# Another layout for the first two chunks' alpha, k and q, turned by identity products, with a new order for the opening fifth

## The chip, the cores and the metric

The kernel runs on one core of a Trainium2 chip. The metric is the time of one execution in microseconds (us) of device time. A core has five engines that matter here: TensorE (PE, with its weight loads as PEld), VectorE (DVE), ScalarE (ACT), GpSimd (POOL) and SyncE (SP), which issues the transfers (DMAs). Each engine works through its own instructions in program order and waits for the others by semaphores.

## The reference

A gated linear attention runs over 4 batches, 8 heads, 768 tokens and 48 channels. Its output, put together over the heads to 3072 tokens of 384 channels, goes through a two-layer block with a hardswish.

```python
for t in range(S):                                   # S = 768
    state = alpha[:, :, t, :, None] * state + np.einsum('bhd,bhe->bhde', k[:, :, t], v[:, :, t])
    y[:, :, t] = np.einsum('bhd,bhde->bhe', q[:, :, t], state)
...
x = np.ascontiguousarray(attn_out.transpose(0, 2, 1, 3)).reshape(B * S, H * D)   # 3072 x 384
h = x @ w_in                                         # w_in 384 x 2048
relu6 = np.clip(h + 3.0, 0.0, 6.0)
g = h * relu6 / 6.0
return (g @ w_out).astype(np.float32)                # w_out 2048 x 384
```

The two weight matrices are given as 64-bit floats and reach the kernel as raw bits; the kernel itself makes 32-bit floats of them.

## The kernel before

**Tiling.** The tokens are cut into 24 chunks of 128, six to a batch; chunk `j` belongs to batch `j // 6`. The recurrence within a chunk is done by cumulative products of alpha (scans along the tokens), so alpha, k and q are needed with channels on the partitions and tokens along the row: two heads of 64 rows each (48 channels and 16 rows of padding) fill the 128 partitions, and four such pairs lie side by side. Two chunks make a group of 256 tokens for the two-layer block.

**Loads.** For chunks 0 to 5 (`FIRST = 6`) `load_akq` (L253) brings alpha, k or q of a chunk in one transfer: partition = token, and on it eight heads of 48 channels, each in a place of 64 (L256). The buffers are the three rings of `rings` (L87): ring `j % 3` for chunk `j`. The 16 pad columns of each head are set once at the start, to 1 for alpha and 0 for k and q (L91); ring 0 by VectorE, rings 1 and 2 by GpSimd. From chunk 6 on the loads go another way, through `quads` (L264), four transfers per tensor, and VectorE turns blocks of 32 by 32 (L288).

**Turning.** `transposed` (L276) puts channels on partitions: for each of the four pairs of heads one TensorE transpose of 128 tokens by 128 rows, into one PSUM bank (L284).

**Order.** The kernel writes the order of its work out by hand as one long list of words, each a step of one chunk, group or weight slice, handed to `run` (L768). Each step issues its instructions at once, so the list fixes the order of every engine's instructions and of SP's transfers. The words that matter here, with their engine and line (the number after the dot is the chunk, the slice or the group):

- `la`, `lk`, `lq`: loads of alpha, k, q (SP, L256); `lv`: the two loads of v (SP, L274); `w`: load of one of sixteen weight slices (SP, L162 for the first matrix, L166 for the second)
- `ta`, `tk`, `tq`: the turning (TensorE, L284; from chunk 6 on VectorE, L288)
- `ca`: turned alpha to its place (ScalarE, L302); `r`: scan backwards, with a reciprocal (VectorE, L311, L315); `p`: scan forwards (VectorE, L322); `k`, `q`: k and q times those scans (VectorE, L334)
- `kb`: k back to tokens on partitions (TensorE, L393); `ck`: copy of it (ScalarE, L397); `u`: products for the state (TensorE, L452); `sm`: next state (VectorE, L460, L462); `st`: decayed state (GpSimd, L428); `sv`: state to its place (ScalarE, L438; the first of a batch by a memset on GpSimd); `qa`: q to its place (ScalarE, L385)
- `sc`: scores (TensorE, L365); `m`: masked scores (VectorE, L375); `ya`, `yb`: attention output (TensorE, L478); `cy`: copy of it (ScalarE, L487)
- `d1`, `d2`, `dx` (ScalarE, L186, L196, L191), `d3` (VectorE, L203 to L210), `d4` (GpSimd, L217): the five parts of turning one weight slice into 32-bit floats; `pd`: pads of `quads` (GpSimd, L251)
- `fa`, `fb`, `f`, `fr`, `fg`, `b`: the two-layer block of the first two groups, done directly (TensorE L512, L501, L539; ScalarE L517; VectorE L521)
- `y`, `xc`, `x`, `s` (VectorE) and `M`, `P` (TensorE, L623, L726), `G`, `K`, `n`, `o`: from the second group on, the two matrix products with sums and differences of blocks, which need fewer products
- `z`: products of the identity by itself into an unused PSUM bank, as many as the last number says (TensorE, L555). Nothing reads them. There are 26 of them, all in the opening.

An fp32 product appears in the trace as two matmul instructions; a transpose as one.

The list begins so:

```python
run("""z.0.5 z.0.3 z.0.1 qa.0.0 w.0 d2.0 d3.0 la.0 ta.0.0 z.0.8 lk.0 tk.0.1 la.1 ta.1.2
       lq.0 tq.0.3 lk.1 lv.0.0 d1.0 ca.0 r.0 p.0 k.0 kb.0.0 z.0.2 z.0.2 q.0 la.2 dx.0 ca.1
       r.1 ck.0 u.0.2.1 sm.0.0 qa.0.1 sv.0.1 tk.1.0 p.1 sc.0.2.3 w.2 lq.1 sm.0.1 k.1 m.0
       ta.2.0 z.0.2 d1.2 ca.2 d2.2 kb.1.0 ck.1 r.2 tq.1.2 q.1 dx.2 lv.1.1 u.1.3.1 z.0.3
       ...
       ya.0.3 yb.0 sc.1.0.2 m.1 ...
```

Of the kernel before, what the change touches and what calls it, by code (L numbers as in the profile page):

```python
# [17 lines left out]
def kernel(  # L18
# [32 lines left out]
    nc = tc.nc  # L51
    B, H, S, D = q.shape
# [8 lines left out]
    G = 2  # L61
# [11 lines left out]
    ident = consts.tile([C, C], FP, tag="ident")  # L73
# [8 lines left out]


    NR = 3
    NV = 3
    ring = {}
    rings = consts.tile([C, 3 * NR, H, 64], FP, tag="rings")  # L87
    for r in range(NR):
        for name, pad in (("a", 1.0), ("k", 0.0), ("q", 0.0)):
            t = ring[name, r] = rings[:, 3 * r + "akq".index(name)]  # L90
            (nc.vector if r == 0 else nc.gpsimd).memset(t[:, :, D:64], pad)  # L91

    vs, As = [], []
    for r in range(NV):
        t = consts.tile([C, 2, H, 64], FP, tag=f"v{r}", name=f"v{r}")
# [10 lines left out]
    for r in range(2):  # L106
        t = consts.tile([C, NP * W + 1], FP, tag=f"ax{r}")
        nc.vector.memset(t, 0.0)
        aX.append(t)
        t = consts.tile([C, NP * W], FP, tag=f"ini{r}")  # L110
# [7 lines left out]
    st, half_st, sm = (consts.tile([C, NP, D], FP, tag=name, name=name)  # L118
                       for name in ("st", "s1", "sm"))
# [109 lines left out]
    def bank(name, j, i):  # L229
        ps_t[name, j] = banks[i].rearrange("r (p n) -> r p n", p=NP)  # L230
        return ps_t[name, j]
# [3 lines left out]
    V = C // BLK  # L235
# [3 lines left out]
    for r in range(NQ):  # L239
        for name in "akq":  # L240
            quads[name, r] = consts.tile([C, NP, V, D], FP, tag=f"{name}q{r}",
                                         name=f"{name}q{r}")

    def rows(t, j):
        b, c = divmod(j, NC)
        return t[b, :, c * C : (c + 1) * C, :]
# [5 lines left out]

    def load_akq(name, j):  # L253
        src = rows({"a": alpha, "k": k, "q": q}[name], j)
        if j < FIRST:
            nc.sync.dma_start(out=ring[name, j % NR][:, :, 0:D],  # L256
                              in_=src.rearrange("h s d -> s h d"))
            return
        to = quads[name, j % NQ]
        to = to.rearrange("r p v d -> r p (v d)")  # L260
        t = src.rearrange("(p a) (u v) d -> a u p (v d)", a=2, v=V)
        for o in range(4):
            skip = BLK * (o % 2)
            nc.sync.dma_start(out=to[BLK * o : BLK * (o + 1), :, 0 : V * D - skip],  # L264
                              in_=t[o // 2, :, :, skip : V * D])
# [10 lines left out]
    def transposed(name, j, i=None):  # L276
        if j >= FIRST:
            t = (K_t if name == "k" else Q_t)[j] = (Ks if name == "k" else Qs)[j % 2]
            by_blocks(t, name, j)
            return  # L280
        t = bank("t" + name, j, i)
        src = ring[name, j % NR]
        for p in range(NP):
            nc.tensor.transpose(  # L284
                t[:, p], src[:, 2 * p : 2 * p + 2].rearrange("s h d -> s (h d)"), ident)

    def by_blocks(to, name, j):
        nc.vector.transpose(out=to.rearrange("r p (u v) -> r p v u", v=V),  # L288
                            in_=quads[name, j % NQ][:, :, :, 0:BLK])
# [305 lines left out]
    for i in range(8):  # L595
        r, o = divmod(i, 3)
        spots.append(raws[r].rearrange("p n w -> p (n w)").bitcast(FP)[:, o * QB : (o + 1) * QB])
    xc = consts.tile([C, len(X_SUMS), C], FP, tag="xc")
# [47 lines left out]
    def hidden1(g, o):  # L646
# [16 lines left out]
    b = {(i, k): w2[:, i * HF : (i + 1) * HF, k * HD : (k + 1) * HD]  # L663
         for i in range(2) for k in range(2)}
    spare = rings.rearrange("r n h e -> r (n h e)").rearrange(
        "r (x f n) -> r x f n", x=3, n=HD)
    t = {1: b[0, 1], 2: spare[:, 0], 3: spare[:, 1], 4: spare[:, 2]}
# [76 lines left out]
    def store2(g, i):  # L744
# [5 lines left out]

    steps = {
        "la": lambda j: load_akq("a", j), "lk": lambda j: load_akq("k", j),
        "lq": lambda j: load_akq("q", j), "lv": load_v, "pd": pad, "w": load_weight,
        "d1": round_low, "d2": magnitude, "dx": sign, "d3": high_bits, "d4": add_low,
        "ta": lambda j, *i: transposed("a", j, *i), "tk": lambda j, *i: transposed("k", j, *i),
# [12 lines left out]
    def run(words):  # L768
        for word in words.split():
            name, *at = word.split(".")  # L770
            steps[name](*(int(x) for x in at))

    with tc.manual_schedule():
        run("""z.0.5 z.0.3 z.0.1 qa.0.0 w.0 d2.0 d3.0 la.0 ta.0.0 z.0.8 lk.0 tk.0.1 la.1 ta.1.2
               lq.0 tq.0.3 lk.1 lv.0.0 d1.0 ca.0 r.0 p.0 k.0 kb.0.0 z.0.2 z.0.2 q.0 la.2 dx.0 ca.1
               r.1 ck.0 u.0.2.1 sm.0.0 qa.0.1 sv.0.1 tk.1.0 p.1 sc.0.2.3 w.2 lq.1 sm.0.1 k.1 m.0
               ta.2.0 z.0.2 d1.2 ca.2 d2.2 kb.1.0 ck.1 r.2 tq.1.2 q.1 dx.2 lv.1.1 u.1.3.1 z.0.3
               lq.2 w.1 lk.2 d4.0 lk.3 la.3 la.4 w.3 lq.3 lv.2.2 lk.4 w.5 pd.0 sv.0.0 pd.1 st.1
               sm.1.0 p.2 d3.2 sm.1.1 ya.0.3 yb.0 sc.1.0.2 m.1 d4.2 sv.1.1 cy.0 qa.1.1 sv.1.0 d1.1
               st.2 d2.1 dx.1 fa.0.1 tq.2.1 q.2 tk.2.3 k.2 fa.2.0 sc.2.0.2 d3.1 m.2 d4.1 ta.3.1  # L780
               ta.4.3 kb.2.0 qa.1.0 ca.3 r.3 ca.4 r.4 ya.1.2 yb.1 tk.3.1 fa.1.2 p.3 k.3 qa.2.1
               qa.2.0 cy.1 d2.3 d3.3 fb.2 fb.1 tq.3.1 q.3 sv.2.0 d1.3 ck.2 u.2.3.2 sm.2.0 d4.3
               fr.0.2.0 tk.4.0 d2.5 sv.2.1 k.4 sm.2.1 st.3 fg.0.2 d3.5 w.6 lv.3.0 lq.4 w.7 fb.0
               sc.3.1.3 m.3 kb.3.2 kb.4.0 f.0.3.3 ya.2.1 ck.3 d1.5 d4.5 d1.6 d2.6 d3.6 d4.6 sv.3.0
               qa.3.1 fr.0.1.0 fr.0.3.1 la.5 yb.2 u.3.3.2 sm.3.0 fg.0.3 fg.0.1 sm.3.1 f.0.5.0
               tq.4.3 f.0.6.3 ta.5.2 cy.2 ck.4 d2.7 qa.3.0 d1.7 d3.7 d4.7 fr.0.5.1 fr.0.0.0 sv.3.1
               fg.0.0 fg.0.5 p.4 ya.3.0 yb.3 f.0.7.2 qa.6.0 qa.12.0 qa.18.0 lq.7 w.4 d2.4 cy.3
               fr.0.6.1 w.9 d2.9 ca.5 d1.9 d1.4 dx.4 la.6 w.8 d3.4 lk.5 w.10 d3.9 ca.6 q.4 fg.0.6
               d4.9 w.12 d2.8 st.4 f.1.1.1 f.1.7.0 sc.4.0.2 f.1.3.3 qa.4.0 d1.8 fr.0.7.0 r.6 d3.8
               d4.8 d4.4 fg.0.7 m.4 fr.1.1.0 fr.1.7.1 fg.1.7 fg.1.1 d2.10 d1.10 f.1.0.2 d2.12 d3.10  # L790
               r.5 d4.10 fr.1.0.0 fr.1.3.1 fg.1.3 fg.1.0 d3.12 f.1.6.0 f.1.2.1 la.8 lq.5 lv.4.1
               w.11 w.13 lq.6 u.4.1.0 tk.5.3 sm.4.0 sv.4.0 d1.12 qa.4.1 d4.12 fa.4.3 fr.1.2.0
               fr.1.6.1 d2.11 d2.13 f.1.4.2 d1.11 sm.4.1 fg.1.2 k.5 kb.5.1 tq.5.3 d3.11 p.5 d4.11
               tq.6 fg.1.6 q.5 p.6 d3.13 d1.13 st.5 la.7 w.15 lv.5.0 lk.6 w.14 ck.5 b.0.0.1 fb.4
               ya.4.2 qa.5.1 sv.4.1 yb.4 sc.5.0.3 fr.1.4.1 cy.4 u.5.2 b.0.1 f.1.5.0 fr.0.4.0 d1.15
               sv.5.0 qa.5.0 lv.12.1 lk.7 lv.6.2 sv.12.0 sv.6.0 d4.13 xc.2.0 fg.1.4 q.6 xc.2.2
               sm.5.0 fg.0.4 ca.7 tk.6 sv.5.1 d2.15 d2.14 d1.14 d3.15 fr.1.5.1 d3.14 k.6 d4.14
               d4.15 fg.1.5 m.5 b.0.2 b.1.0.2 b.1.1 kb.6.0 ya.5.3 yb.5 b.1.2 cy.5 P.1.0.0 P.1.1.3
               lq.8 K.1.0 ck.6 u.6.2.3 b.1.3 bo.1 b.0.3 tq.7 y.5 y.1 y.3 y.0 y.6 x.0 y.9 y.7 xc.2.1
               y.11 y.13 y.2 y.8 xc.2.3 x.1 s.1.0.0 s.1.1.1 x.2 tk.7 y.10 s.1.2.3 G.1.0.0 y.4  # L800
               sm.6.0 P.1.3.3 xc.2.4 s.1.3.2 P.1.2 sc.6.2.1 y.16 y.12 y.15 s.1.4 r.7 y.17 y.19
               xc.2.5 y.20 s.1.5 xc.2.7 y.14 y.18 y.21 xc.2.6 y.23 lq.9 so.1 lv.7.0 lk.9 bo.0 K.1.2
               K.1.1 P.1.4 M.2.0.1 P.1.5 n.2.0.8 M.2.1 n.2.1.9 G.1.1.1 M.2.7.2 n.2.7.11 sv.6.1
               sm.6.1 k.7 G.1.2.2 xc.2.10 x.3 xc.2.8 p.7 q.7 st.7 y.22 xc.2.9 m.6 M.2.15.3 M.2.2
               n.2.2.10 M.2.8 kb.7.0 M.2.3 M.2.4 P.1.6 qa.7.0 ck.7 n.2.4.12 G.1.3.3 O.1.0 la.9 lk.8
               ca.9 o.2.0.0 M.2.9 u.7.1.2 ya.6.0 e.2.0.0 qa.6.1 yb.6 lv.8.2 cy.6 y.24 r.9 o.2.1.0
               M.2.10 M.2.5 n.2.10.14 e.2.1.1 n.2.5.13 sm.7.0 h.2.0 tq.8 ca.8 tk.8 h.2.1 M.2.6.0
               M.2.11 M.2.18.1 sc.7.0.3 sv.7.1 qa.7.1 n.2.11.15 n.2.18.10 sv.7.0 M.2.12 M.2.16
               M.2.19 n.2.12.12 M.2.13 sm.7.1 r.8 m.7 o.2.3.0 ya.7.3 n.2.13.12 yb.7 cy.7 M.2.14
# [8 lines left out]
               n.3.11.8 e.3.5.0 M.3.12 n.3.12.10 q.9 O.2.0 kw.9 la.11 kr.8 kr.9 ca.11 up.8.0.1  # L818
               sp.8.2.3 M.3.13 M.3.15.0 M.3.16 G.2.2.0 o.3.3.0 sm.8.0 mp.8 o.3.4.0 sm.8.1 r.10
               sv.8.1 n.3.13.10 M.3.14 P.2.4 o.3.6.1 o.3.7.0 M.3.6.3 qa.8.0 qa.9.0 qa.8.1 sv.8.0  # L820
               st.9 e.3.4.1 lk.11 lq.11 O.1.2 la.12 lq.10 G.2.1.2 P.2.6 sm.9.0 h.3.4 sm.9.1 o.3.2.0
               ya.8.1 sv.9.1 sv.9.0 qa.9.1 st.10 G.2.3.3 yb.8 ya.9.3 yb.9 M.3.17 P.3.0.1 tk.11
               o.3.2.1 o.3.3.1 tk.10 h.3.5 O.2.2 O.2.3 la.13 lv.10.2 sv.10.0 cy.8 e.3.2.1 cy.9
               xc.4.0 xc.4.1 xc.4.3 h.3.2 xc.4.4 xc.4.5 o.3.7.1 M.4.0.0 e.3.6.0 e.3.3.1 h.3.3
               P.3.1.2 e.3.7.1 n.4.0.10 K.3.0 h.3.6 xc.4.6 h.3.7 xc.4.7 k.10 M.4.7.3 M.4.1 n.4.1.13
               tq.10 s.3.1.11 s.3.0.9 G.3.0.0 kt.10 xc.4.8 xc.4.10 s.3.2.12 r.11 p.10 P.3.3.2 M.4.2
               n.4.2.14 n.4.7.15 K.3.2 s.3.3.9 k.11 q.10 s.3.5 kt.11 p.11 s.3.4 P.3.2 M.4.3 M.4.4
# [128 lines left out]
```

## Time and profile before

| | |
|---|---|
| median of 3 runs | 530.81 us (529.37 to 530.86) |
| the profiled execution | 530.19 us, of which its span 528.4 us |
| TensorE busy | 519.6 us, 98% of the span |
| VectorE busy | 471.7 us, 89% |
| ScalarE busy | 257.9 us, 49% |
| GpSimd busy | 49.7 us, 9% |
| moved by DMA | 54.40 MB; 83,328 of 124,100 packets under 512 bytes |
| first load of alpha | issued at 1.24 us, landed 5.48 us later |
| first scan on VectorE | starts at 8.59 us |

Times in the trace count from the start of the span. The timeline lists instructions in order of time, with the idle time of the engine before them and what ended it. The chain of waits is followed back from the last instruction: at each step to what released it, or to the instruction before it on its engine. A table by stretches gives each engine's busy time within a window. A matmul's duration holds its way through the array; matmuls follow one another faster than that, so work is counted by the spacing of instructions in a full stream.

### The profile page before, as it was taken

The numbers are of one execution on the slowest core, as the hardware profiler recorded it, in microseconds if no ns is written. First come the engines' busy times: TensorE is split into PE (matmuls) and PEld (weight loads), VectorE is DVE, ScalarE is ACT, GpSimd is POOL, SyncE is SP. The second block draws the span as 40 slices with busy tenths as digits, with TensorE's granted clock in tenths as the row PEclk, the third lists the DMA queues.
The fourth block names the chain that finished last, engine by engine and source line by source line (L and its number), as shares of the span: only waits on it lengthen the run. The fifth ranks groups of instructions, "written<-read, shape, count | busy, mean of one in ns | idle before, by whom it ended". The sixth has DMA issues, their size and how long they took to land.

```text
span 528.4 us, 15020 instructions
## 1 busy us (share of the span) xinstructions
PE 519.6 (98%) x6300; PEld 495.6 (94%) x6300; DVE 471.7 (89%) x817; ACT 257.9 (49%) x503; POOL 49.7 (9%) x71
## 2 busy tenths in 40 slices
PE   7899999999999999999999999999999999999997
PEld 7788887779999999999999999999999999999997
DVE  6999999999999999999999999999999996276471
ACT  4889866013653643652544536543444545344330
POOL 6323342100000000000000100000000000000000
PEclk9999999999999999999999999999999999999999
DMA  9999987140026535355555453454163150010001
GB/s 173 222 254 265 245 242 170 29 119 1 17 58 140 131 84 120 78 110 125 123 114 133 98 117 75 111 120 118 30 139 92 30 121 13 2 31 8 9 1 45
DMA packets 124100, 54.40 MB, mean 103 GB/s; under 512 B 83328, under 2 KB 116864, under 8 KB 124032
## 3 DMA queue, kind: packets, MB, share of 16 engines
q1 hardware_dynamic: 124032, 53.44, 44.7%
q8 instruction: 49, 0.80, 0.7%
q14 instruction: 19, 0.16, 0.1%
HBM read 44.50 MB, written 8.91 MB: 101 GB/s over the span
## 4 chain that ended last, share of the span: by engine, by line
PE 81%; DVE 12%; ACT 2%; DMA 2%; issue 2%; POOL 0%; SPq 0%; DVEq 0%; ACTq 0%
PE m_ps L726 37%; PE m_ps L623 35%; PE t_ps L478 4%; PE t_ps L365 2%; PE t_ps L452 2%; DVE g_sb L521 1%; DMA rings<-in_alpha_dram 1%; DVE w L208 1%; DVE raw L210 1%; PE m_ps L555 1%; DVE w L207 1%; DVE P L322 1%; DMA qq<-in_q_dram 1%; DVE A L375 1%; PE t_ps L284 1%
## 5 line engine op out<-in xcount | busy, mean ns | idle before, releaser
L726 PE MATMUL m_ps<-w,g_sb 128*128 128x192 f32 x704 | 121.6, 326 | 0.2 <-DVE oh L742 0.2
L629 ACT COPY g_sb<-m_ps 128x512 f32<-128x512 f32 x110 | 63.5, 585 | 115.4 <-PE m_ps L623 95.1
L726 PEld LDWEIGHTS m_ps<-w,g_sb 128*128 128x128 f32 x704 | 113.8, 190 | 1.2 <-DVE oh L742 0.8
L726 PE MATMUL m_ps<-rings,g_sb 128*128 128x192 f32 x528 | 91.6, 326 | 0.8 <-DVE g_sb L670 0.8
L726 PEld LDWEIGHTS m_ps<-rings,g_sb 128*128 128x128 f32 x528 | 85.3, 190 | 1.1 <-DVE g_sb L670 1.1
L623 PE MATMUL m_ps<-xc,w 128*128 128x128 f32 x640 | 83.5, 278 | 0.0
L517 ACT ACTIVATE r<-g_sb,half 128x512 f32<-128x512 f32 x80 | 56.5, 721 | 49.1 <-DVE g_sb L564 22.8
L623 PEld LDWEIGHTS m_ps<-xc,w 128*128 128x128 f32 x640 | 77.8, 192 | 1.5 <-ACT g_sb L629 0.2
L521 DVE SCALAR_TENSOR_TENSOR g_sb<-r,g_sb 128x512 f32<-128x512 f32 x80 | 53.8, 683 | 4.6 <-ACT r L517 4.4
L623 PE MATMUL m_ps<-xT,raw 128*128 128x128 f32 x400 | 52.2, 276 | 0.0
L623 PEld LDWEIGHTS m_ps<-xT,raw 128*128 128x128 f32 x400 | 48.9, 192 | 0.2
L670 DVE TENSOR_TENSOR g_sb<-g_sb 128x512 f32<-128x512 f32 (+1 forms) x55 | 42.1, 792 | 2.6 <-PE m_ps L726 2.5
L428 POOL TENSOR_TENSOR st<-sm,R 128x192 f32<-128x192 f32 x20 | 12.1, 606 | 337.3 <-DVE sm L462 254.6
L623 PE MATMUL m_ps<-xT,w 128*128 128x128 f32 x320 | 41.7, 276 | 0.0
L623 PEld LDWEIGHTS m_ps<-xT,w 128*128 128x128 f32 x320 | 38.7, 192 | 0.2
L385 ACT COPY A<-q 48x256 f32<-48x256 f32 x88 | 35.5, 403 | 6.0 <-DVE q L334 4.7
L560 DVE TENSOR_TENSOR g_sb<-g_sb 128x512 f32<-128x512 f32 x40 | 27.0, 681 | 6.7 <-ACT g_sb L629 6.6
L501 PE MATMUL m_ps<-xT,w 128*128 128x256 f32 x144 | 32.5, 381 | 0.0
L623 PE MATMUL m_ps<-xc,raw 128*128 128x128 f32 x240 | 32.0, 276 | 0.0
L501 PEld LDWEIGHTS m_ps<-xT,w 128*128 128x128 f32 x144 | 26.9, 190 | 3.8
L311 DVE TENSOR_TENSOR_SCAN R<-t,ones 128x516 f32<-128x516 f32 x24 | 29.5, 1230 | 0.6 <-ACT t L302 0.6
L623 PEld LDWEIGHTS m_ps<-xc,raw 128*128 128x128 f32 x240 | 29.7, 192 | 0.2
(105 smaller groups left out, 722.1 us busy)
## 6 DMA issues: line engine op xcount, KB each, us to landing
raw<-in_moe_w_out_dram SPq DMA_DIRECT2D x8, 768.0 KB, 5.9
raw<-in_moe_w_in_dram SPq DMA_DIRECT2D x6, 768.0 KB, 6.3
v<-in_v_dram SPq DMA_DIRECT2D x48, 96.0 KB, 3.2
out_dram<-oh SPq DMA_DIRECT2D x44, 96.0 KB, 2.0
far<-kq SPq DMA_DIRECT2D x64, 64.0 KB, 2.2
kb<-far SPq DMA_DIRECT2D x64, 64.0 KB, 2.1
qq<-in_q_dram SPq DMA_DIRECT2D x36, 96.0 KB, 2.6
aq<-in_alpha_dram SPq DMA_DIRECT2D x36, 96.0 KB, 2.7
```

Source lines behind the costliest of these rows:

```text
L311: nc.vector.tensor_tensor_scan(out=reverse(R, n - 1, n), data0=reverse(ax, n, n), data1=reverse(ones, n, n), initial=0.0, op0=ALU.mult, op ...
L385: nc.scalar.copy(out=to[:, a], in_=Q_t[j][64 * a : 64 * a + D, :, half])
L428: nc.gpsimd.tensor_tensor(out=st, in0=sm, in1=R_t[j][:, :, 0:1].to_broadcast([C, NP, D]), op=ALU.mult)
L478: nc.tensor.matmul(y_of(j, (i + 1) // 2, p)[:, HB * b : HB * b + HB], vb[:, p, e : e + 32], A_t[j][:, b, 2 * p + a], start=(b == 0 and i = ...
L501: nc.tensor.matmul(h[:, f], w1[:, kk, o : o + C], xT_t[g][:, kk], start=(kk == 0), stop=(kk == KT - 1))
L517: nc.scalar.activation(out=to, in_=h, func=AF.Relu, bias=half, scale=1.0 / 6.0)
L521: nc.vector.scalar_tensor_tensor(out=to, in0=r, scalar=1.0, in1=h, op0=ALU.min, op1=ALU.mult)
L560: eng.tensor_tensor(out=out, in0=in0, in1=in1, op=ALU.add if s1 > 0 else ALU.subtract)
L623: nc.tensor.matmul(acc[g][i][:, f * C : (f + 1) * C], spots[w][:, f * C : (f + 1) * C], x_of(g, x), start=(first and f == 0), stop=last, s ...
L629: nc.scalar.copy(out=slots[z], in_=acc[g][i])
L670: nc.vector.tensor_tensor(out=out, in0=in0, in1=in1, op=ALU.subtract)
L726: nc.tensor.matmul(to[g], a, rhs[:, f], start=(first and f == 0), stop=(last and f == HF - 1), skip_group_check=True)
```

## The change

**Loads.** For chunks 0 and 1 (`QUADS = 2`) a partition now holds four successive tokens of two heads: partition `4u + p` has tokens `4u` to `4u + 3` of heads `2p` and `2p + 1`, so that each run in memory is 4 tokens of 48 channels (768 bytes) instead of one (192 bytes). It is still one transfer per tensor, of 192 KB in all, and fills the first 384 columns of the ring.

**Turning.** For each of the four tokens and each of the two heads of a pair, one fp32 product of 64 columns of the ring (48 channels, and 16 more that lie behind them) with the identity: 64 rows of PSUM by 128 columns, written with a stride of four so that the tokens come out in order. Eight products take the place of four transposes, for alpha, k and q of chunks 0 and 1. The 16 columns behind the last head are set by six more small memsets, three on VectorE and three on GpSimd.

**Order.** The words of the opening (about the first third of the list's text, a fifth of the time) are arranged anew, and `sv.12.0` moves a little further back. The words are the same as before, none more and none fewer.

```diff
+    QUADS = 2
...
             (nc.vector if r == 0 else nc.gpsimd).memset(t[:, :, D:64], pad)
+            if r < QUADS:
+                (nc.vector if r == 0 else nc.gpsimd).memset(t[:, 6, 0:16], pad)
...
     def load_akq(name, j):
         src = rows({"a": alpha, "k": k, "q": q}[name], j)
+        if j < QUADS:
+            to = ring[name, j % NR].rearrange("r h e -> r (h e)")[:, 0 : 2 * V * D]
+            nc.sync.dma_start(out=to.rearrange("r (a x) -> r a x", a=2),
+                              in_=src.rearrange("(p a) (u v) d -> u p a (v d)", a=2, v=V))
+            return
...
         t = bank("t" + name, j, i)
         src = ring[name, j % NR]
+        if j < QUADS:
+            src = src.rearrange("s h e -> s (h e)")
+            for v in range(V):
+                for a in range(2):
+                    o = D * (V * a + v)
+                    nc.tensor.matmul(
+                        t[64 * a : 64 * a + 64].rearrange("r p (u v) -> r v u p", v=V)[:, v],
+                        src[:, o : o + 64], ident, start=True, stop=True)
+            return
...
+        run("""z.0.5 qa.0.0 la.0 ta.0.0 lk.0 tk.0.1 la.1 ta.1.2 z.0.3 ca.0 r.0 k.0 p.0 kb.0.0 ca.1
+               r.1 w.1 lq.0 tq.0.3 z.0.1 lv.0.0 lk.1 la.2 w.0 q.0 lq.1 w.2 lv.1.1 lq.2 lk.2 w.3
+               la.4 la.3 d1.1 ck.0 u.0.2.1 tk.1.0 z.0.8 d2.1 qa.0.1 dx.1 d2.0 d1.0 d3.1 sm.0.0
+               sc.0.2.3 p.1 sm.0.1 k.1 m.0 d3.0 z.0.2 ta.2.0 ca.2 sv.0.1 r.2 z.0.2 tq.1.2 kb.1.0
+               z.0.2 d4.1 st.1 sv.0.0 sv.1.0 ck.1 dx.0 u.1.3.1 sm.1.0 q.1 sm.1.1 p.2 qa.1.1 z.0.3
+               ya.0.3 yb.0 sc.1.0.2 m.1 cy.0 d2.2 d1.2 dx.2 tk.2.3 tq.2.1 q.2 k.2 d3.2 pd.0 d4.0
+               ...
+               P.1.0.0 K.1.0 d4.14 s.1.1.1 tq.6 m.5 y.3 y.6 y.1 k.6 sm.5.0 y.5
+               sv.5.1 s.1.0.0 fg.0.4 y.7 P.1.1.3 b.1.2 b.0.2 b.1.3 ya.5.3 yb.5 kb.6.0 ck.6 y.2
+               s.1.4 s.1.3.2 y.11 x.0 y.4 G.1.0.0 y.16 y.10 y.8 x.1 x.2 s.1.2.3 P.1.2 P.1.3.3 y.0
+               ...
```

## The prediction

> **What bounds the kernel now.** I read the page's busy shares first, then the timeline of the opening, then the chain of waits, then busy time by stretches. The page:
>
> ```profile
> PE 519.6 (98%) x6300; PEld 495.6 (94%) x6300; DVE 471.7 (89%) x817; ACT 257.9 (49%) x503; POOL 49.7 (9%) x71
> PE   7899999999999999999999999999999999999997
> DVE  6999999999999999999999999999999996276471
> ```
>
> TensorE is busy almost throughout, and the holes lie in the first slices. So the end of the program is the moment from which TensorE never stops, plus the work then left. The timeline says when that is (columns: start, duration, engine, line, operation, count, idle time before and its releaser):
>
> ```profile
> 1.24 0.48 SPq L256 DMA_DIRECT2D rings<-in_alpha_dram  x1
> 6.85 1.09 PE L284 MATMUL t_ps<-ident,rings 128*128 128x128 f32 x4 [1.18 <-DMA rings<-in_alpha_dram]
> 7.73 3.23 PE L555 MATMUL m_ps<-ident 128*128 128x128 f32 x16
> 7.97 0.59 ACT L302 COPY t<-t_ps 128x512 f32<-128x512 f32 x1 [0.75 <-PE t_ps L284]
> 8.59 1.23 DVE L311 TENSOR_TENSOR_SCAN R<-t,ones 128x516 f32<-128x516 f32 x1 [0.32 <-ACT t L302]
> ...
> 19.46 0.57 PE L452 MATMUL t_ps<-v,kb 64*48 64x48 f32 x32 [0.29 <-issue]
> 19.96 0.94 PE L555 MATMUL m_ps<-ident 128*128 128x128 f32 x6
> 20.83 1.10 PE L478 MATMUL t_ps<-A,v 128*32 128x64 f32 x64
> 28.63 0.66 PE L393 MATMUL t_ps<-ident,k 128*128 128x128 f32 x4 [0.27 <-DVE A L375]
> ```
>
> Alpha of chunk 0 lands 5.48 us after its issue, and transpose, copy and first scan follow at once. L555 is the filler (`z`). The last filler ends at 20.83, where `ya.0` starts; from there TensorE has real work. Add up the steps from `ya.0` to 110.67 by their spacing in a full stream (each half of an fp32 product: 0.116 us for 128 columns, 0.224 for 256, 0.336 for 384, 0.163 for 192; transposes 0.11), and there are 88.85 us of work in 89.84 us, so 1.0 us of holes. From 110.90 on the chain of waits is TensorE without a break, but for 0.77 us near 370. Before 110.90 the same chain runs mostly over VectorE, which is nearly as full:
>
> ```profile
> 20.83:110.67 89.84, 89.33 (x1089) 72.67 (x1088) 87.34 (x138) 60.22 (x103) 27.95 (x21) 1.00 0.79 189
> ```
>
> (Columns: PE, PEld, DVE, ACT, POOL busy, clock, DMA share, GB/s.) VectorE's last steps ahead of the unbroken stretch, in the timeline:
>
> ```profile
> 109.79 0.67 DVE L670 TENSOR_TENSOR g_sb<-g_sb 128x512 f32<-128x512 f32 x1
> 110.49 0.36 DVE L742 TENSOR_TENSOR oh<-m_ps,p 128x192 f32<-128x192 f32 x1
> ```
>
> So a gain can come from two places only: `ya.0` (and `kb.2`, which waited for `m.2`) earlier than 20.83 (28.63), and at most 1.0 us of holes behind it. A shorter transfer by itself is worth nothing.
>
> One more thing is read from half-microsecond stretches of TensorE:
>
> ```profile
> 9.50:10.00 0.50, 0.50 (x4) 1.00 1.55 164
> 10.50:11.00 0.50, 0.50 (x6) 1.00 1.40 157
> 11.50:12.00 0.50, 0.50 (x8) 1.00 1.50 163
> ```
>
> The granted clock reads 1.00, yet a 128-column instruction takes 0.217 us (18 fillers in 3.91 us) until about 10.5 and 0.11 to 0.12 afterwards. The fillers from 1.47 to 5.68 did not bring the fast rate; those from 7.73 brought it after 2.8 us.
>
> **The change, part by part.** The profiled execution took 530.19 us (span 528.4); the median of the runs, 530.81, is 0.6 above it. I sum against 530.19.
>
> *The loads.* 1,024 packets of 192 bytes become 256 of 768. During the small packets the trace shows 163 GB/s (1.2 us for 196 KB), with larger ones 385 to 418 (0.5 us). Six loads save some 4 us of DMA time. More important for `la.0`: `w.0` (786 KB, 2 us at 390 GB/s) no longer goes ahead. `la.0` now overwrites pad columns, so its issue waits for two memsets on VectorE (0.88 to about 1.1), and lk.0, la.1 and w.1 are queued behind it on SP; the issue stays at about 1.24. Landing: the nearest rows are 64 KB in 2.2 us and 96 KB in 2.6 us (medians of issues), and 4.0 us, the shortest landing of an L256 load. I take 2.9, nearest to the 96 KB row: landed at 4.1 instead of 6.72. Bounds 3.4 to 5.2. The six small memsets cost about 0.06 us each on VectorE and 0.1 on POOL, ahead of work that waits anyway: nothing.
>
> *The turning.* Four transposes (0.44 us fast, 0.88 slow) become eight products, that is 16 instructions of 64 output partitions by 128 columns. The trace has none of this shape. One after the other they would take 16 x 0.116 = 1.86 us (3.5 slow). The `attend` rows (L478: 32 output partitions, all 128 rows, alternating column groups) run 64 instructions of 64 columns in 1.03 us, 16 ns each, where 64 columns alone would need 58: nearly four side by side. Scaled to 128 columns that is 0.53 us as the lower bound. I take two side by side, since two groups of 64 fill the array: 0.93 us, 1.75 slow. In sum 6 x 0.5 = 3 us more TensorE work, all ahead of `ya.0`, hidden while fillers and waits stand there.
>
> [...]
>
> *The order, to the first scan.* The filler before `ta.0` shrinks from nine to five products and ends at 1.47 + 10 x 0.217 = 3.64. `ta.0` runs 4.2 to 5.95, plus 0.24 of drain (1.12 us from start to copy now, against 0.88 of issue); copy 0.59; first scan at 6.85 instead of 8.59. But `d3.0` (1.4 us) was done before 8.59 and now comes later, so VectorE is really only 0.35 us ahead.
>
> *To `m.0`.* I take the fast rate 2.8 us after 4.2, at 7.0. Then `tk.0` ends at 7.35, `ta.1` at 8.3, three fillers 9.0, `kb.0` 9.5, `tq.0` 10.4. VectorE: r.0 to 8.26, k.0 8.9, p.0 10.1, r.1 11.5, q.0 12.1, d3.1 13.45, sm, p.1 14.95, sm, k.1 15.9, m.0 17.4, without a wait. Now `m.0` ends at 18.13 with `d3.0` in the place of `d3.1`: 0.7 earlier.
>
> *ScalarE to `ya.0`.* In the new queue `ck.1` stands behind ca.1, d1.1, ck.0, d2.1, qa.0.1, dx.1, d2.0, d1.0, ca.2, sv.0.1, sv.1.0. qa.0.1 waits for q.0 (12.15); then 0.82 + 1.76 + 0.81 + 0.85 + 0.49 + 0.72 + 0.72 + 0.59, with a wait of some 0.1 for POOL (d4.1, 2.5 us from 14.7, stands ahead of st.1): 19.0. `u.1` to 19.65, filler 0.85: `ya.0` at 20.5 instead of 20.83. All TensorE waits for this queue.
>
> *To the shared order.* `kb.2` follows `m.2`; from `m.0` to `m.2` both orders hold the same VectorE work, so it moves 0.5 to 0.7 earlier. Up to the first `P` product that starts the unbroken chain, the new order asks VectorE for 97.8 us of steps (through s.1.2.3) instead of 102.3 (through G.1.0.0), by row durations: sums for late use were moved back. TensorE has moved 3.3 us (b.0.3, u.6) behind that point, so 1.2 us of room is left, and I credit 0.3 us of the holes. Weights land earlier, not later: no cost.
>
> Sum: 0.6 + 0.3 = 0.9 us less, 529.3.
>
> **Rivals.** *Everything early:* alpha lands at 3.4, as quickly as the 64 KB rows, and the holes close. First scan 0.7 earlier still, 1.3 at `m.2`, 0.9 of holes: 528.0. For: VectorE waits nowhere up to `m.0`. Against: the SP issue and the first memsets don't move. [...]
>
> *Slower: one product at a time.* Place: ta.0, tk.0, ta.1, tq.0. Then first scan at 8.25, ca.1 to 11.9, tq.0 at 14.3, q.0 to 14.9 instead of 12.1: `m.0` at 20.2, 2.1 us behind now, and no hole large enough to give it back: 532.2, and 533 if the slow rate lasts to 10.5. It decides as soon as one tensor takes over 1.4 us at the fast rate. For: no row of this shape; against: L478.
>
> *The load is not what counts:* 256 packets land as slowly as the 4.0 us row (5.2). Everything to `m.0` is 1.1 later, the gain is gone: 530.2. The same comes of a slow rate to 10.5: tq.0 at 12.2 holds q.0, `m.0` at 18.1.
>
> **How the numbers follow.** Forecast 0.50, early 0.15, one at a time 0.18, no effect 0.17. About 0.3% (1.6 us) is what a measurement of this kernel can tell from no change. Against the median, faster means under 529.2: half of the forecast's half, and the early case: 0.39. Slower, over 532.4: the one-at-a-time case with its slow rate, and waits not foreseen in a new order: 0.18. The rest, 0.43, is the same. The range goes from 527.6 (early, and the hole near 370 partly) to 532.8. The forecast's own is 528.6 to 530.4.
>
> **What would show it.** `ta.0` starts near 4.2, sixteen product instructions per tensor in under 1 us once fast; first scan near 6.85; q.0 without a TensorE wait; the last filler ends near 20.5, `kb.2` near 28.0; holes behind it under 1 us. Wrong if a tensor's products take 1.9 us, if ScalarE reaches `ck.1` after 19.5, or if TensorE waits for VectorE between 30 and 110.

## The result, and the profile after

The changed kernel takes 536.49 us (median of 4 runs, 535.25 to 539.99) against 530.59 for the kernel before (4 runs on the same chip): 1.0133 times, 95% interval 1.0104 to 1.0162. It is 5.9 us slower, where 529.3 was forecast and the range ended at 532.8. The profiled execution is the longest of the four, 539.99 us with a span of 538.2.

First the page of the changed kernel: the busy shares, then the rows of the slices.

```profile
PE 525.6 (98%) x6372; PEld 500.6 (93%) x6372; DVE 472.4 (88%) x820; ACT 257.5 (48%) x503; POOL 52.4 (10%) x74
PE   8689999999999999999999999999999999999997
DVE  7769999999999999999999999999998996367471
PEclk9979999999999999999999999999999999999999
```

TensorE has 72 more matmuls (and 72 more weight loads) and is busy 6.0 us longer. The third slice, 26.9 to 40.4 us, is new: TensorE busy for 8 tenths where it was 9, and a granted clock of 0.7 where it was full. The timeline says what happens there (columns as before; L260, L296, L301, L328, L382, L469, L495, L529 and L572 are the old L256, L284, L284, L311, L365, L452, L478, L512 and L555; L296 are the new products, L301 the remaining transposes):

```profile
1.07 0.76 SPq L260 DMA_DIRECT2D rings<-in_alpha_dram  x1
4.33 4.16 PE L296 MATMUL t_ps<-ident,rings 128*64 128x128 f32 x48 [0.36 <-DVE ones L118]
6.96 1.23 DVE L328 TENSOR_TENSOR_SCAN R<-t,ones 128x516 f32<-128x516 f32 x1 [2.71 <-ACT t L319]
...
16.82 1.09 PE L296 MATMUL t_ps<-ident,rings 128*64 128x128 f32 x16
17.85 0.66 PE L410 MATMUL t_ps<-ident,k 128*128 128x128 f32 x4
...
19.68 0.82 PE L469 MATMUL t_ps<-v,kb 64*48 64x48 f32 x32 [0.73 <-DMA v<-in_v_dram]
20.44 0.94 PE L572 MATMUL m_ps<-ident 128*128 128x128 f32 x6
21.30 1.10 PE L495 MATMUL t_ps<-A,v 128*32 128x64 f32 x64
22.33 0.68 PE L382 MATMUL t_ps<-q,k 48*64 48x64 f32 x26
28.27 0.48 PE L382 MATMUL t_ps<-q,k 48*64 48x64 f32 x6 [5.26 <-issue]
```

The opening goes as forecast: products at 4.33, first scan at 6.96 instead of 8.59. Then, in the middle of the scores of chunk 1 (`sc.1.0.2`, 32 matmuls of one step, with no wait between them), TensorE stops after 26 of them and stands for 5.26 us. The releaser is "issue": no semaphore, so neither data nor another engine was awaited. It is the longest wait of TensorE in the kernel; the groups of waits (total, times, longest) say so:

```profile
PE t_ps L382 <- issue: 5.3, 1, 5.3
PE m_ps L572 <- POOL ident masks.py:199: 1.5, 1, 1.5
PE t_ps L469 <- DMA v<-in_v_dram: 0.7, 1, 0.7
```

What follows the hole is slow as well. By stretches (columns PE, PEld, DVE, ACT, POOL, clock, DMA share, GB/s), and in the timeline:

```profile
25.00:30.00 5.00, 1.73 (x12) 1.61 (x12) 1.13 (x4) 3.08 (x4) 0.00 (x0) 0.76 1.17 241
30.00:35.00 5.00, 5.00 (x28) 4.98 (x26) 2.97 (x6) 0.00 (x0) 1.56 (x1) 0.56 0.73 203
21.30:120.26 98.96, 93.42 (x1078) 78.36 (x1078) 89.37 (x139) 59.03 (x101) 30.48 (x25) 0.97 0.64 156
```

```profile
30.45 4.72 PE L529 MATMUL m_ps<-xT,w 128*128 128x128 f32 x24
37.09 0.66 PE L410 MATMUL t_ps<-ident,k 128*128 128x128 f32 x4 [0.27 <-DVE A L392]
```

28 matmuls between 30 and 35, where the kernel before had 67. The trace has the granted clock at 0.50 from 27.56 to 34.39 us. The third row is a stretch from `ya.0` on with about as many matmuls (1078) as the one to 110.67 shown of before (1089): there 0.5 us without TensorE at work, here 5.5. `kb.2` starts at 37.09 instead of 28.63, 8.46 later: 0.47 from `ya.0` (21.30 for 20.83), 5.53 in the hole, and 2.46 because the rest up to `kb.2` takes 8.82 us after the hole, and took 6.36 from the same matmul before. The last matmul of `P` is issued 9.83 us later (535.06 for 525.23); 7.84 of that is there at the fortieth matmul of `M`, and 1.2 comes between 160 and 180 us, where TensorE waits for VectorE (L704) and ScalarE (L646). VectorE is late there because it waited for the store of an earlier output, whose buffer it fills next (L759 is the old L742):

```profile
165.66 0.36 DVE L759 TENSOR_TENSOR oh<-m_ps,p 128x192 f32<-128x192 f32 x1 [0.98 <-DMA out_dram<-oh]
```

The kernel before has no such wait. The other three executions have a mean granted clock of 0.997 instead of 0.994, which would fit a slow stretch half as long, though no profile shows where theirs lay; they are 3 to 4.7 us shorter than the profiled one.

One more row of the trace counts, a kind of transfer that the program did not write. In half a microsecond of each kernel (22.5 to 23.0 before; 25.5 to 26.0 after; packets, MB, share of the engines):

```profile
q8 instruction: 1, 0.02, 17.0%
```

```profile
q8 instruction: 1, 0.02, 13.3%
```

The page of the changed kernel counts 50 such packets, 0.82 MB in all, so 16 KB each; and TensorE has 6372 matmuls and 6372 weight loads, 255 for each packet; the kernel before, with 144 of these instructions less, has 49, so 257 for each. These are taken to be TensorE's own instructions, in blocks of 256, which the stops below bear out. That is the theory that was tested: **TensorE runs out of instructions**, because the block with the next ones is fetched late, behind the data. Its rivals were that the new order's transfers are late (weights, v, q), that the products are too slow, and that the halved clock alone is at work.

### The profile page after: what moved, and what is told of

Read it like the earlier page. It is cut to its first block, busy times and chain, and to the rows that moved or that the text cites. A ratio compares the mean times of both kernels' runs of the same rounds, so it can differ in the third digit from the quotient of the medians.

```text
span 538.2 us, 15166 instructions
## 1 busy us (share of the span) xinstructions
PE 525.6 (98%) x6372; PEld 500.6 (93%) x6372; DVE 472.4 (88%) x820; ACT 257.5 (48%) x503; POOL 52.4 (10%) x74
## 4 chain that ended last, share of the span: by engine, by line
PE 80%; DVE 8%; DMA 4%; SPq 4%; issue 2%; ACT 1%; DVEq 0%; ACTq 0%
PE m_ps L743 32%; PE m_ps L640 27%; PE m_ps L518 6%; PE t_ps L495 4%; PE m_ps L556 4%; PE m_ps L529 2%; PE t_ps L382 2%; DMA v<-in_v_dram 2%; PE t_ps L469 2%; DVE g_sb L577 1%; SPq L432 1%; DMA kb<-far 1%; PE t_ps L301 1%; DVE g_sb L538 1%; SPq L440 1%
## 5 line engine op out<-in xcount | busy, mean ns | idle before, releaser
L646 ACT COPY g_sb<-m_ps 128x512 f32<-128x512 f32 x110 | 63.5, 585 | 114.3 <-PE m_ps L640 96.8
L445 POOL TENSOR_TENSOR st<-sm,R 128x192 f32<-128x192 f32 x20 | 13.6, 681 | 342.6 <-DVE sm L479 225.5
L328 DVE TENSOR_TENSOR_SCAN R<-t,ones 128x516 f32<-128x516 f32 x24 | 29.2, 1218 | 2.7 <-ACT t L319 2.7
L339 DVE TENSOR_TENSOR_SCAN P<-t 128x516 f32<-128x516 f32 x24 | 31.0, 1291 | 0.0
```

Of the source, the lines that this page charges most:

```text
L328: nc.vector.tensor_tensor_scan(out=reverse(R, n - 1, n), data0=reverse(ax, n, n), data1=reverse(ones, n, n), initial=0.0, op0=ALU.mult, op ...
L339: nc.vector.tensor_tensor_scan(out=P_t[j], data0=aX[j % 2][:, 0:n], data1=ini[j % 2], initial=0.0, op0=ALU.mult, op1=ALU.add)
L646: nc.scalar.copy(out=slots[z], in_=acc[g][i])
```

## The experiments

The medians are set against runs of the kernel before on the same chip (529.9 to 530.7 us). Where an expectation names another instruction as the moment at which a block is asked for, the table behind the experiments replaces it. In e2, e3, e4, e5, e8, e9 and e10 the time came out above the range that the theory gave, in e12 it is the rival's: the theory told where TensorE stops better than what a run takes, since other waits and a lowered clock came on top.

**e1: the new loads and products with the order of before.** The changed kernel with the old list handed to `run`.

> The new loads and the identity products, in the order of before. Theory (TensorE runs out of instructions: a block of 256 is asked for when the one before begins, and its transfer waits behind the data queued then): the 144 additional TensorE instructions bring the asking for the third block from 21.9 us forward to about 18.5 us, and the block is used up at about 22 instead of 28 us; how long the fetch waits depends on what is queued at 18.5, so a small hole of 0 to 2 us is possible: 530 to 533 us. Rival (the new order alone is at fault, by a late transfer or a wrong sequence): no hole, 530 us or a little less, since alpha lands earlier.

532.59 us, 1.0041 (1.0025 to 1.0057): a third of the loss. The hole is there at the same record, but short:

```profile
PE t_ps L382 <- issue: 0.8, 1, 0.8
```

Its profile loses 0.75 us by the first `M` product and 1.3 more near 160 us, where VectorE waits 1.1 us for an output's store, as after the change.

**e2: the new order alone.** `QUADS = 0`, so loads and transposes as before.

> The new order with the loads and transposes of before. Theory (instructions run out): 144 fewer TensorE instructions, so the third block is asked for at about 22.4 instead of 20.4 us and needed only at about 28; a fetch that waits 5 us is still in time, no hole of 5 us and no halved clock: 529 to 532 us. Rival (the order is at fault): the hole stays, 535 to 537 us.

533.02 us, 1.0048 (1.0033 to 1.0063). No stop for instructions; instead two waits for transfers that the new order put behind weight slices (`lq.0` behind `w.1`, `lv.1` behind `w.0` and `w.2`):

```profile
PE t_ps L301 <- DMA rings<-in_q_dram: 2.8, 1, 2.8
PE t_ps L469 <- DMA v<-in_v_dram: 1.7, 1, 1.7
```

The clock was at 0.50 from 11.71 to 15.12, behind the first of them. The two halves give +1.9 and +2.4, the whole +5.9: they make each other worse by 1.6.

**e3: fewer instructions.** Everything as changed, but each tensor turned by four products of 128 columns in place of eight of 64, so that 96 fewer instructions (matmuls and weight loads) stand ahead.

```diff
-                for a in range(2):
-                    o = D * (V * a + v)
...
+                o = D * v
+                nc.tensor.matmul(t.rearrange("r p (u v) -> r v u p", v=V)[:, v],
+                                 src[:, o : o + C], ident, start=True, stop=True)
```

> The changed kernel, with four products of 128 columns in the place of eight of 64 for each tensor: same time on TensorE (8 instructions of 0.109 us against 16 two by two), 96 instructions fewer in all. It leaves out the right turning of the second head of each pair. Theory (instructions run out): third block asked for at about 21.7, needed at about 27, so the hole shrinks from 5.3 us to under 1.5 us and the clock is not halved: 529 to 532 us. Rival (the turning's TensorE time or the order is at fault): unchanged, 535 to 537 us.

533.08 us, 1.0042 (1.0024 to 1.0059). No hole and no lowered clock: 3.4 us less than the change. What is left is as much as e2's.

**e4: the data out of the fetch's way.** `w.3`, `la.4`, `la.3` and `w.6` issued behind `w.5`, which itself waits for `d4.0`.

```diff
-  lq.2 lk.2 w.3 la.4 la.3 d1.1 ck.0 ... pd.0 d4.0 st.2 d4.2 d1.3 qa.1.0 w.6 lv.2.2 lk.3 w.5 lq.3
+  lq.2 lk.2 d1.1 ck.0 ... pd.0 d4.0 w.5 w.3 la.4 la.3 st.2 d4.2 d1.3 qa.1.0 w.6 lv.2.2 lk.3 lq.3
```

> The changed kernel, with the loads w.3, la.4, la.3 and w.6 moved behind w.5, which waits for d4.0 until about 23 us; TensorE's instructions are the same. Theory (the fetch waits behind queued data): little is queued when the third block is asked for at 20.4, the fetch starts by 22 instead of 25.9 us, the hole at 23 us is gone and the clock is not halved; weights come later, which may cost 1 to 2 us: 529 to 533 us. Rival (the hole has nothing to do with the queue): hole as before, 535 us or more.

538.25 us, 1.0137 (1.0114 to 1.0159): no faster, but the parts tell. The fetch starts at 22.09 instead of 25.86 and the hole shrinks from 5.26 to 1.72 us; and the alpha held back is now late itself:

```profile
PE t_ps L301 <- DMA rings<-in_alpha_dram: 3.6, 2, 3.4
PE t_ps L382 <- issue: 1.7, 1, 1.7
```

Behind that wait the clock was at 0.50 from 33.13 to 36.55. So the length of the hole depends on the data in front of the fetch, and moving that data buys one wait with another.

**e5 and e10: the instructions alone.** The kernel before, with as many more instructions as the change has and nothing else: products of 32 x 32 with one column of the identity (`zt`, into the same unused bank). In e5 44 of them stand in the place of eight fillers, ahead of `tk.0`.

```diff
-  la.0 ta.0.0 z.0.8 lk.0 tk.0.1
+  la.0 ta.0.0 zt.0.44 lk.0 tk.0.1
```

> The kernel before, with its eight fillers after ta.0 replaced by 44 tiny identity products of 32 by 32 by one column: TensorE gets 144 instructions more at that place, as the change gave it, and nothing else changes, neither loads nor order. Theory (instructions run out): TensorE stops after its 705th instruction, in sc.1 at about 22.3 us, with no semaphore to wait for; the fetch, asked for at 19.8, comes behind the queue at 22 to 23 us, so a hole of 1 to 3 us: 531.5 to 534 us. Rival (the hole belongs to the new loads or the new order): no hole, 530 to 531 us.

538.51 us, 1.0166 (1.0144 to 1.0188). The hole is there ("PE t_ps L365 <- issue", 2.1 us), but the clock was at 0.50 from 9.73 to 16.56 and from 26.80 to 33.62, so this kernel loses time in a second way, and its 8.6 us are not the hole's alone. That is why e10 adds 36 of them behind `sc.0`, where nothing of the clock changes:

```diff
-  p.1 sc.0.2.3 w.2 lq.1
+  p.1 sc.0.2.3 zt.0.36 w.2 lq.1
```

> The kernel before with all its fillers, and 36 tiny identity products (144 instructions) more, right after sc.0, where TensorE waits 1.2 us for VectorE anyway. Nothing else changes. Theory (instructions run out): TensorE stops after its 705th instruction in sc.1, as in e5, but without e5's lower clock ahead of it; ya.0 within 0.5 us of 20.8, a hole of 1 to 3 us at 22 to 23 us: 531 to 534 us. Rival (e5 lost its time by the clock alone): no hole, 530 to 531 us.

536.64 us, 1.0104 (1.0082 to 1.0126), with the clock at 1.00 from 10.09 us to the end. The kernel before, with its own loads, transposes and order, stops as the change does, after 26 of the 32 score products:

```profile
22.01 1.10 PE L478 MATMUL t_ps<-A,v 128*32 128x64 f32 x64
23.04 0.68 PE L365 MATMUL t_ps<-q,k 48*64 48x64 f32 x26
25.46 0.34 PE L365 MATMUL t_ps<-q,k 48*64 48x64 f32 x6 [1.75 <-issue]
```

The tiny products themselves make `ya.0` 1.2 us later (22.01), and its profile loses another 1.5 us near 165, behind a wait of 1.3 us for an output's store; so not all of the 6 us is the hole's. But the hole needs neither the new layout nor the new order: the number of instructions ahead is enough.

**e6: still more instructions.** The changed kernel with 33 tiny products in place of eight fillers: 100 more.

```diff
-  tk.1.0 z.0.8 d2.1
+  tk.1.0 zt.0.33 d2.1
```

> The changed kernel, with its eight fillers before sc.0 replaced by 33 tiny products: 100 TensorE instructions more. Theory (instructions run out): the third block is asked for at about 17 instead of 20.4 us, and the transfers have a lull at 18.5 to 19.5 us in which the fetch can run, before it is needed at 21.8; so more instructions take the hole at 23 us away and the clock is not halved: 529.5 to 533 us, the rest depending on the fourth block (asked for at 22.5, needed at 28). Rival (simply too many instructions or too much TensorE work): as slow as the change or slower, 536 us or more.

532.95 us, 1.0047 (1.0021 to 1.0073): 100 instructions more than the change, and 3.5 us faster than it. The stop in `sc.1` is gone; a smaller one stands a block earlier, in `sc.0`:

```profile
15.21 0.74 PE L382 MATMUL t_ps<-q,k 48*64 48x64 f32 x21
17.49 0.69 PE L382 MATMUL t_ps<-q,k 48*64 48x64 f32 x11 [1.53 <-issue]
```

Against what was expected, the clock was at 0.50 here too, from 15.45 to 22.28, and still the kernel is faster. If the number of instructions or the work on TensorE were what costs, more of it would not help: it is where the block ends that counts.

**e7: is `ya.0` what sets the end?** The kernel before without the three fillers ahead of `ya.0`.

```diff
-  lv.1.1 u.1.3.1 z.0.3
+  lv.1.1 u.1.3.1
```

> The kernel before without its last filler (z.0.3, six instructions, 0.86 us ahead of ya.0). If the end is set by when ya.0 starts, as the prediction had it, the program ends up to 0.8 us earlier: 529.8 us. If VectorE's m.1 and m.2 set kb.2, TensorE waits there instead, kb.2 stays near 28.6 and the time is the same within 0.1%.

529.46 us, 0.9991 (0.9976 to 1.0006), no difference, and `kb.2` starts at 28.71, as before (28.63). But `ya.0` itself hardly moved, because it now waits for VectorE's next state (`sm`) where the filler stood:

```profile
20.74 1.10 PE L478 MATMUL t_ps<-A,v 128*32 128x64 f32 x64 [0.52 <-DVE s L462]
```

So this run shows that the filler ahead of `ya.0` cost nothing. It does not test what an earlier `ya.0` would be worth, and its interval reaches from 1.3 us less to 0.3 us more.

**e8 and e9: taking instructions out.** e8 is e1 without 13 of the fillers (52 instructions less).

```diff
-  ta.0.0 z.0.8 ... kb.0.0 z.0.2 z.0.2 q.0 ... ta.2.0 z.0.2 d1.2 ... u.1.3.1 z.0.3
+  ta.0.0 z.0.4 ... kb.0.0 q.0 ... ta.2.0 d1.2 ... u.1.3.1
```

> The new loads and products in the order of before, with 13 of the fillers taken out (8 after ta.0 become 4, those before q.0, after ta.2 and before ya.0 go): 52 TensorE instructions fewer than in e1. Theory (instructions run out): third block asked for at 21, needed at 25.8, so the hole of 1.05 us at 22.3 that e1 has is gone: about 1 us less than e1, 530.5 to 531.7 us. Rival (e1 loses its time elsewhere): as e1, 532.6 us.

532.54 us, 1.0056 (1.0033 to 1.0078). No stop for instructions, and yet as slow as e1. Where e1 lost 1.05 us in the hole, VectorE here waits 1.1 us for the turning of q of chunk 1:

```profile
DVE q L351 <- PE t_ps L296: 1.1, 1, 1.1
```

That turning took nearly twice its time (1.98 us for 1.10 in e1), because the granted clock was at 0.50 from 18.10 to 21.51; in e1, with its fillers, it stayed at 1.00 there:

```profile
18.23 1.98 PE L296 MATMUL t_ps<-ident,rings 128*64 128x128 f32 x16
...
113.39 2.87 PE L743 MATMUL m_ps<-w,g_sb 128*128 128x192 f32 x16 [1.45 <-DVE oh L759]
```

`kb.2` is 0.90 later than in the kernel before, the first `P` step 1.28, the third (113.39) 2.49. That one waits for VectorE, which lost more on its way: 0.5 us waiting for ScalarE (54.92), and 0.84 at 81.99, where a step of 0.56 us takes 1.40 while GpSimd's memsets (L451) run. Three of the four other executions have a mean clock of 1.00 and take 531.5 to 534.7 us, so the clock alone does not explain this run.

e9 is the changed kernel without 15 fillers, with `lq.0` ahead of `w.1`, `lv.1` ahead of `w.0`, and `w.6` behind `lk.3`.

```diff
-  w.1 lq.0 tq.0.3 z.0.1 lv.0.0 lk.1 la.2 w.0 q.0 lq.1 w.2 lv.1.1 lq.2
+  lq.0 w.1 tq.0.3 lv.0.0 lk.1 la.2 lv.1.1 w.0 q.0 lq.1 w.2 lq.2
```

> The changed kernel with its order mended where the trace shows it late: lq.0 ahead of w.1, lv.1.1 ahead of w.0, w.6 behind lk.3, and 15 of the fillers taken out (60 TensorE instructions fewer). Theory (instructions run out, the rest is late transfers): third block asked for about 1 us later in the list and needed 60 instructions later, so the hole at 23 us falls from 5.3 to some 1 to 2 us, u.1 no longer waits for v, the clock is not halved: 530 to 533 us. Rival (the new order costs 2 to 3 us in its VectorE sequence whatever the transfers do): 533 to 535 us.

535.32 us, 1.0084 (1.0052 to 1.0116). No stop of over 0.2 us at a block's end, but with its fillers gone the clock was at 0.50 from 12.8 to 16.2 and from 23.1 to 29.9, and TensorE waited 2.1 us for ScalarE's `ck.0`, which stands behind `d1.1` and so behind `w.1`, now later. Three loads were moved and 15 fillers taken out at once: this run says little on either.

**e11 and e12: what could be kept.** The new layout and the products for alpha alone, in the order of before (`if j < QUADS and name == "a"`), 48 more instructions.

> The order of before, with the new layout and products for alpha of chunks 0 and 1 alone (48 TensorE instructions more than before instead of 144). Theory (instructions run out): third block asked for at about 21 us, needed at about 26, no hole at 22 to 23: 530 to 531.5 us. Rival (the loads or products cost by themselves): over 531.5 us, near e1's 532.6.

530.01 us, 0.9997 (0.9979 to 1.0015): no difference. Its profile has no hole, `ya.0` at 20.24 and `kb.2` at 28.03, 0.6 earlier than before, and its span is 0.7 shorter (527.7 for 528.4). The interval, from 1.1 us less to 0.8 more, can neither show nor exclude a gain of that size; and its fillers went at 0.11 us from 4.5 us on, those of before only from 10.5, so the 0.6 us need not be the layout's. e12 goes on from there: alpha's load ahead of `w.0`, its turning after five fillers, and `d2.0 d3.0 d1.0` behind the first scan.

```diff
-  z.0.5 z.0.3 z.0.1 qa.0.0 w.0 d2.0 d3.0 la.0 ta.0.0 z.0.8 ... d1.0 ca.0 r.0 p.0
+  z.0.5 qa.0.0 la.0 w.0 ta.0.0 z.0.3 z.0.1 z.0.8 ... ca.0 r.0 d2.0 d3.0 d1.0 p.0
```

> As e11 (new layout and products for alpha alone, order of before), but alpha of chunk 0 is issued ahead of w.0, ta.0 comes after five fillers instead of nine, and d2.0, d3.0 and d1.0 stand behind the first scan. Theory (a load that lands early moves the opening as long as TensorE has its instructions): first scan near 7.0 instead of 8.2, d3.0 done in the time until k lands, ya.0 up to 0.8 us earlier than in e11, no hole at 22 us: 529 to 530 us. Rival (k of chunk 0, now behind w.0 and in small packets, sets the pace): ya.0 as in e11 or later, 530 to 531 us.

530.27 us, 1.0012 (0.9993 to 1.0031): no difference either, although its first scan comes 2.05 us earlier than in the kernel before:

```profile
6.54 1.23 DVE L328 TENSOR_TENSOR_SCAN R<-t,ones 128x516 f32<-128x516 f32 x1 [2.34 <-ACT t L319]
...
20.92 1.10 PE L495 MATMUL t_ps<-A,v 128*32 128x64 f32 x64
...
28.62 0.66 PE L410 MATMUL t_ps<-ident,k 128*128 128x128 f32 x4 [0.27 <-DVE A L392]
```

`kb.2` is where it was: `d3.0` and the rest of VectorE's work only moved behind the scan. No kernel that was run is faster than the one before by more than its interval.

**All traces together.** Number TensorE's records (matmuls, weight loads, its semaphore instructions) in order of time. The holes are all behind record 449 or 705, that is 193 and one or two times 256. In the fourteen traces (of before, after and twelve experiments) the first fetch never starts sooner than 0.69 us after record 193, nor the second sooner than 0.99 us after record 449. That fits, for these two, a block asked for when the block ahead of it is entered. As a rule the traces do not show it: counted on in the same way, the seventh fetch starts 0.37 us ahead of its record before the change and 0.63 after it. The rows for the second fetch, with one for the first fetch of e6:

| kernel | work from record 449 to 705 | fetch starts, after 449 | takes | stop behind 705 | resumes after the end of the fetch |
|---|---|---|---|---|---|
| before | 6.13 us | 1.61 us | 1.36 us | none | - |
| after | 3.11 | 6.18 | 1.06 | 5.48 | 1.34 |
| e1 | 2.86 | 1.59 | 1.04 | 1.05 | 1.29 |
| e2 | 5.66 | 2.93 | 1.46 | 0.39 | - |
| e3 | 5.86 | 2.97 | 1.45 | none | - |
| e4 | 3.10 | 2.45 | 1.27 | 1.93 | 1.31 |
| e5 | 2.89 | 2.37 | 1.45 | 2.28 | 1.34 |
| e6 (193 to 449) | 4.05 | 3.61 | 1.03 | 1.84 | 1.26 |
| e8 | 4.98 | 0.99 | 0.94 | 0.52 | - |
| e10 | 3.05 | 2.30 | 1.43 | 1.97 | 1.28 |
| e11 | 5.79 | 1.39 | 1.46 | none | - |

(Stops from the start of record 705 to that of the next; e7, e9 and e12, left out, have 0.54, 0.11 and 0.04. In all of these up to 0.54 the next block had come before TensorE went on.) In all six kernels that stop for long, TensorE goes on 1.26 to 1.34 us after the end of the fetch, however long it stood. So the stop is the start, the fetch and 1.3 us, less the time that the block's work lasts: 6.18 + 1.06 + 1.34 - 3.11 = 5.47 for the change (5.48 measured), 1.59 + 1.04 + 1.29 - 2.86 = 1.06 for e1 (1.05). For the kernel before, 4.3 against 6.13: nothing. Two things came together. The 144 instructions shifted the end of a block, so that one block holds just the quickest instructions: `u.1` (64 records), six filler matmuls (12), `ya.0` (128) and 52 of `sc.1`, 256 in all, done in 3.1 us. And the new order had the data queued in front of the fetch (6.18 us to its start; 1.6 with the order of before).

## Why the prediction was wrong

*What held.* The first load landed at 4.19 (4.1 forecast) and the products start at 4.33 (4.2). Two products of 64 output partitions do run side by side: sixteen instructions from 16.82 to the next shape at 17.85, 1.03 us for 0.93 forecast, where one at a time would be 1.86. So the second rival fell. Weight loads ran beside them as well: one of 0.14 us starts at 17.10, while the pair of products that started at 17.09 runs (0.27 us). The first scan came at 6.96 (6.85), `m.0` ended at 17.05 (17.4; 18.13 before). VectorE was ahead, as the sum said. That the fast rate came at 7.08 (7.0) was luck: the fillers of before, which the prediction read, sped up at about 10.4 (where the trace's clock has its first entry, which is why it reads 1.00 ahead of it), the same fillers in the same order at 4.8 in e7; and with the opening of the change unaltered up to `ca.0`, the granted clock rose at 5.21 in e6 and 5.83 in e4.

*What was mis-sized.* `ya.0` came at 21.30, not 20.5: `u.1` waited until 19.68 for v of chunk 1, issued at 10.54 and landed 9.01 us later. "Weights land earlier, not later: no cost" looked at the weights alone. Moved ahead, they delayed what was queued behind them, `lv.1` here and `lq.0` in e2 (TensorE waits 2.8 us for it). Without a stop for instructions this order costs some 2.4 us (e2 and e3). The 0.3 us credited for holes behind `kb.2` cannot be read off, as 5.5 us without TensorE stand there.

*The step that failed* is "In sum 6 x 0.5 = 3 us more TensorE work, all ahead of `ya.0`, hidden while fillers and waits stand there." The time was hidden; the number was not. The 144 instructions were costed as time on the array, and never as a stream that has to be fetched, and "holes behind it under 1 us" counted only waits of engines for each other. The row that carries the price, "q8 instruction", stood in the trace of before and has no term in the sum. Of the 5.9 us, about 3.4 go with the stop and the halved clock behind it (536.49 against 533.08 in e3, which has neither); how those two divide in a run that was not profiled stays open.

*The gain stays unproven.* The 0.9 us hung on `ya.0` and `kb.2` coming earlier. A first scan 2 us earlier alone brought nothing (e12): VectorE, nearly full up to 110 us, has the same work to do before `kb.2`. In e7 `ya.0` hardly moved. In e11 both came 0.6 us earlier and the profiled execution ended 0.7 earlier, as the prediction's rule has it, but its medians cannot tell that from no change.

*Open.* Which packets are served ahead of a fetch. Why e8, with no stop, is still 2.7 us behind also in executions at full clock: its profile shows where VectorE lost the time, and no run isolates it. And why the output's store, for which VectorE waits 1.0 to 1.3 us near 160 us in after, e1 and e10, frees its buffer too late there.

## What to carry to other kernels

Count instructions as well as time: here many short matmuls in a row used up a block of 256 in about 3 us (2.86 in e1, 3.11 in the change). By the table its successor took 8.6 where its fetch waited 6.2 behind weights (the change); where the fetch started within 1.0 to 1.6 us it is an estimated 3.2 (e8) to 4.3 us (before), from their start and fetch and the 1.3 us of the runs that stopped. A wait with the releaser "issue" in the middle of a step that has no wait of its own was the sign (5.26 us in the change, 0.8 in e1); the profile's instruction queue, held against the count of records, shows whether a late block is behind it. Adding or taking out instructions ahead moved such a stop or removed it (100 more in e6, 52 less in e8 than in e1), so compare versions of an opening with that in mind before their order is judged.

## What the runs showed of the hardware

**TensorE's instructions arrived in blocks of 256** over the same DMA engines as the data: 50 packets of 16 KB for 12,744 matmuls and weight loads in the change, one of them with 13.3% of the engines' time in its half microsecond. A late block stopped TensorE for 1.05 to 5.48 us. In the kernel before it stopped nothing, since the block ahead of it lasted 6.13 us and an estimated 4.3 were needed; in the change 3.11 stood against 8.6.

**Behind the longest stop the granted clock was halved.** In the change TensorE stood from 23.01; the granted clock fell to 0.50 at 27.56, 4.6 us on, and stayed there for 6.83 us, 6.1 of them with TensorE at work again (28.27 to 34.39). The halved stretches given above for e2, e4 and e8 lasted 3.4 us, those of e5 and e6 6.8, those of e9 3.4 and 6.8; no run isolates what sets the length. The stops of 1.05 (e1) and 1.97 us (e10) left the clock at 1.00. A long stop is not needed, though: it fell at 18.10 in e8, where no wait of TensorE before was over 1.5 us, and beside or right behind the tiny products at 9.73 in e5 and 15.45 in e6, but not behind those of e10 (1.00 from 10.09 us on).

**At a change of shape TensorE lost about 0.15 us**, in the one place that was read: 1.03 us for the sixteen instructions of a turning up to the next shape (16.82 to 17.85), where pairs follow one another at 0.109 us within it, which makes 0.87 for the eight pairs. The first pair takes 0.05 more than that, the last, up to the next shape, 0.10 more.
